# Hedgehog attention and channel mix: the first batch in halves, with four two-bank PSUM tiles and reuse of tiles ahead of the first mix

## The chip, the cores and the metric

The kernel runs on one core of a Trainium2 chip. The metric is the device time in microseconds (us). A kernel is executed several times, in rounds with the kernel before on the same chip. A run more than 1.5% above the fastest of its kernel counts as slow, and slow runs are left out of the comparisons. A difference of 2% or more counts as faster or slower.

Engine names are those of the profile: PE is TensorE's matmuls, PEld its weight loads, DVE is VectorE, ACT ScalarE, POOL GpSimd, SP SyncE (it issues DMAs). "Half clock" is a stretch in which the profile shows a granted TensorE clock of 0.50. In the kernel before, such a stretch lasts 3.41 us, and in it a product of 512 columns starts every 0.427 us, at full clock every 0.216 us (medians, from start to start).

## The reference, cut to what matters

```python
def phi(x):                                   # q, k: (8, 8, 576, 64), w_phi: (64, 128)
    proj = einsum('bhsd,df->bhsf', x, w_phi)
    proj = proj - max(abs(proj), axis=-1)
    return concatenate([exp(proj), exp(-proj)], axis=-1)
kv  = einsum('bhsf,bhsd->bhfd', phi(k), v);   z = sum(phi(k), axis=2)
x   = (phi(q) @ kv) / (phi(q) . z + 1e-6)     # heads side by side: (8, 576, 512)
xk  = mu_k * x + (1 - mu_k) * x_prev          # x_prev: x moved down by one row, zeros first
xr  = mu_r * x + (1 - mu_r) * x_prev
out = sigmoid(xr @ w_r) * (relu(xk @ w_k) ** 2 @ w_v)     # w_k: (512, 1024)
```

There are 8 batches of 4 head pairs, so 32 pairs, numbered 0 to 31. The channel mix of a batch needs x of all its pairs.

## The kernel before: the parts that matter here

The program defines small groups of instructions, each with a name, and one long list, ORDER, gives the sequence in which they are emitted. Each engine's queue has that sequence, and what stands behind a waiting instruction waits too: GpSimd stood idle 2.80 us until a copy could run at 131.54 us, and a cast behind it, whose input VectorE had written by 130.35 us, ran at 133.10 us. `qp4` is the q product of pair 4, `h0.3` the fourth slice of batch 0's first channel-mix product. `:1` gives the PSUM tile, `/DVE` the engine where there is a choice, and `+3@0` puts three dummy matmuls ("fills") in front. These compute nothing and keep PE busy.

The program held eight PSUM banks, as three two-bank tiles ("P") and two single banks ("M"). A sequence has 576 = 9 x 64 rows; the ninth slot of each q and k, the "tail", is worked on its own:

```python
def tp():   s["ps"] = ps = ptile(A, "ps_e")         # a two-bank tile: k tail in bank 0, q tail in bank 1
def rt_():  ...                                     # DVE: maxima of both banks
def mhe():  ...                                     # POOL: maxima as two bf16 parts
def mte():                                          # PE: their transpose, into a single bank M
    s["pm"] = pm = motile(("mo", "m" + tag), "ps_me")
    nc.tensor.transpose(pm[:, 0:64].bitcast(BF), mh, ident)
def mce(eng): copy(eng, s["mT"], s["pm"][:, 0:64].bitcast(BF))
def kae():  nc.tensor.matmul(s["ps"][:, 0, 0:n*128], ...)                # PE: k tail less its maximum
def ekt():  ... nc.scalar.activation(t, s["ps"][:, 0, 0:n*128], Exp)     # ACT: two exponentials, tk
def qte():                                          # PE: the q tail anew, into a single bank M
    s["pq"] = ps = motile(("mo", "q" + tag), "ps_qe")
    nc.tensor.matmul(ps[:, 0:n*128], lhsT=wph[64:128, :], ...)
def eqe():  ... nc.scalar.activation(t, s["pq"], Exp)                    # ACT: two exponentials, tq
# ... cut ...
def eq(pn):                                         # ACT: exponentials of q, two of 512 for each sign
    for h in range(2):
        nc.scalar.activation(t[:, h, :], s["qT"][:, h], AF.Exp, scale=(1.0 if pn == 0 else -1.0))
```

From pair 8 on, x is transposed by a DMA (`xz`, tile `xs<-x_sc`). A small copy (`xu`), a difference (`df`) and two mixes (`xa`, `xb`) follow, on POOL and DVE.

Of the kernel before, what the change touches and what calls it, by code (L numbers as in the profile page):

```python
# [8 lines left out]
FP = mybir.dt.float32  # L9
BF = mybir.dt.bfloat16  # L10
AF = mybir.ActivationFunctionType
ALU = mybir.AluOpType
# [7 lines left out]
ones ident lv0.0 lv0.0.d:0 lk0.1 lq0.1 lv0.1 dve2 hk hq hk.d:0 lk0.1.d:0 dve3 hq.d:0 lk0.0.d/ACT  # L20
lq0.0.d/DVE lk0.2 lq0.2 pt0:2+9@0 wphi wphi.d:0 mus dve1 lv0.2 lk1.0 pb0/DVE pa0/ACT tr0 tp0.0:2+1@0
rt0.0 mhe0.0 lk0.2.d:0 qp0:1 rq0 lq0.2.d:0 kp0:0 rk0 mte0.0:1+3@0 lq1.0 lq1.0.d:0 lv1.0 mh0
lq0.1.d:0 pt1:1 pa1/DVE mce0.0/ACT kae0.0 lk1.2 lq1.2 lv1.2 pb1/ACT tr1 lq1.2.d:0 qp1:1+2@0 mt0:1
rq1 ekt0.0 mc0/ACT wk.0 pt2:2 ka0 pb2/DVE pa2/ACT kp1:1 rk1 mh1 ea0 pt3:2 pb3/ACT lk1.0.d:0 eb0
pa3/DVE tr3 mt1:1+4@0 mc1/DVE tr2 vc0/POOL wk.1 qp2:2 ka1 ea1 mus.d:0 eb1 rq2 kv0:0 kc0/DVE wr.0
wk.1.d:0 wr.1 lv1.2.d:0 kp2:2+1@0 rk2 wv.0 qt0:0 pt4:1+1@0 lv1.0.d:0 mh2 mt2:1+1@0 qa0 qb0 lk1.2.d:0
pa4/DVE pb4/DVE qte0.0:0 eqe0.0 tp0.1:1 mc2/DVE ka2 tr4 lv0.2.d:0 pt5:0 ea2 rt0.1 mhe0.1
mte0.1:0+1@1 pb5/DVE wv.0.d:0 pa5/DVE eb2 mce0.1/DVE kae0.1+2@1 lv0.1.d:0 ekt0.1 pt6:0 pb6/ACT
pa6/DVE pt7:2 pa7/DVE nd0:1 qt1:0 rd0 pb7/ACT vc1/POOL vc2/POOL vc3/ACT qp3:2 rq3 kp3:1+1@1 wv.1 rk3
mh3 tr6 qa1 qb1 tp0.2:2+3@1 qte0.1:0 tr7 eqe0.1 rt0.2 mhe0.2 kv1:0 kc1/ACT xt0:1 xf0/ACT mt3:0  # L30
mc3/ACT nd1:0 tr5 vc4/POOL xe0/ACT ka3 ea3 eb3 df0/POOL mte0.2:1+1@0 rd1 xt1:0 mce0.2/DVE kae0.2
ekt0.2 tp1.0:0 qte0.2:1 eqe0.2 rt1.0 qp4:1 qt2:2 lk2.0 qa2 qb2 mhe1.0 mte1.0:1 rq4 xa0 kv2:1 kc2/ACT
mce1.0/DVE kae1.0 ekt1.0 vc5/POOL xf1/DVE xb0 qte1.0:1 wr.0.d:0 kp4:2 kv3:1 eqe1.0 kc3/ACT nd2:0 rk4
mh4 mt4:1 rd2 qp5:1 mc4/ACT ka4 rq5 xe1/ACT wk.0.d:0 ea4 eb4 lq2.0 xt2:1 lq2.0.d:0 qp6:0 rq6
df1/POOL xa1 qt3:1+1@0 qa3 kv4:2+1@0 kc4/DVE wk.d xb1 wr.1.d:0 kp5:0 qt4:2+1@0 rk5 qb3 nd3:1 rd3 mh5
xe2/ACT mt5:0+3@0 lk2.0.d:0 tr2.0 xf2/ACT xt3:1 qa4 qb4 mc5/ACT df2/DVE ka5 xe3/ACT xf3/ACT tr2.2
xa2 xb2 wv.1.d:0 ea5 eb5 nd4:2 rd4 df3/POOL xa3 qt5:1 qa5 xb3 kv5:0+3@0 tr2.2.d:0 kp6:2 xt4:1
xf4/ACT xe4/DVE kc5/ACT h0.0:0 h0.1:1 qb5 rl0.0/ACT rl0.1/ACT sq0.0/ACT vc6/POOL vc7/DVE rk6 qp7:1
nd5:0 df4/POOL rq7 mh6 mt6:1 mc6/ACT h0.2:0 rl0.2/ACT qt6:1 qa6 xa4 tr2.0.d:0 wr.d r0.0:1 tr9 xb4
sq0.2/POOL th0.0 tr8 rd5 h0.3:0 qb6 sq0.1/POOL rl0.3/DVE lv2.0 lv2.0.d:0 xt5:1 xf5/DVE xe5/DVE ka6  # L40
kp7:0 h0.4:0 h0.5:1 qp8:1 ea6 df5/POOL eb6 rl0.4/ACT sq0.4/ACT rk7 mh7 sq0.3/ACT kv6:2 rl0.5/DVE
mt7:1 mc7/ACT lk3.0 lq3.0 lv3.0 lk4.0 lq4.0 rq8 lk4.0.d:0 kc6/ACT r0.1:0 th0.1 ka7 ea7 eb7 tr11 tr10
lq3.0.d:0 tp2.0:1 rt2.0 h0.6:1 r0.2:0 rl0.6/DVE sq0.6/ACT th0.2 nd6:2 rd6 h0.7:1 mhe2.0 mte2.0:0
mce2.0/DVE vc8/POOL vc9/POOL kv7:0 kc7/DVE rl0.7/ACT vc10/POOL kae2.0 ekt2.0 qp9:2 rq9 qte2.0:1
xt6:0 sq0.7/POOL qt7:0 lk3.0.d:0 xf6/DVE xe6/DVE eqe2.0 qa7 qb7 kp8:1 rk8 kp9:2 rk9 wv.d sq0.5/POOL
v0.0:0 ob0.0 tr3.0 so0.0 mh8 mt8:1 nd7:0 mc8/ACT ka8 mh9 mt9:0 mc9/ACT xa5 tr3.2 xb5 v0.1:1 rd7
ob0.1 tr3.2.d:0 vc11/ACT ea8 df6/POOL eb8 xa6 xb6 v0.2:0 ob0.2 xt7:1 xe7/ACT xf7/ACT qt8:1 qa8 qb8
df7/DVE xa7 xb7 ka9 lv3.0.d:0 vc12/POOL kv8:0 r0.3:0 tr3.0.d:0 tr13 tr12 lq4.0.d:0 th0.3 v0.3:1
kc8/DVE ob0.3 kp10:0 so0.1 qp10:1 rq10 rk10 ea9 eb9 h1.0:0 h1.1:1 rl1.0/ACT sq1.0/ACT nd8:1 rd8
kv9:2 kc9/ACT h1.2:0 qt9:1 qp11:2 mh10 rq11 rl1.1/ACT xz8 rl1.2/ACT sq1.2/POOL mt10:1 so0.2 mc10/ACT  # L50
sq1.1/POOL h1.3:0 rl1.3/DVE qa9 qb9 r1.0:1 th1.0 sq1.3/POOL kp11:2 rk11 mh11 ka10 ea10 h1.4:0 tr15
eb10 lv4.0 rl1.4/DVE sq1.4/ACT h1.5:1 rl1.5/DVE mt11:0 mc11/DVE so0.3 nd9:1 qp12:0 sq1.5/ACT ka11
xz8.d:0 ea11 eb11 h1.6:0 h1.7:1 vc13/POOL vc14/POOL tr14 vc15/POOL rd9 rq12 xz9 qt10:1 xz9.d:0
rl1.7/DVE rl1.6/DVE lk5.0 kv10:2 kc10/DVE tp3.0:0 sq1.7/POOL rt3.0 qa10 mhe3.0 qb10 r1.1:1 th1.1
he0.0:0 rle0.0/DVE nd10:1 r1.2:1 sq1.6/ACT mte3.0:0 mce3.0/ACT rd10 xz10 xz10.d:0 qt11:2 th1.2
kp12:1 xu8/POOL df8/DVE xa8 so0.0.d:0 kae3.0 xu9/POOL qa11 qb11 rk12 v1.0:1 ob1.0 mh12 ekt3.0
he0.1:0 mt12:1 mc12/ACT xb8 kv11:2 lv4.0.d:0 so0.1.d:0 tr4.0 df9/DVE rle0.1/ACT kc11/ACT qp13:0
qte3.0:1 sqe0.0/DVE eqe3.0 xu10/POOL df10/POOL ka12 kp13:2 so0.2.d:0 so0.3.d:0 so1.0 ea12 so1.0.d:0
r1.3:0 eb12 rq13 rk13 nd11:0 rd11 th1.3 v1.1:1 xz11 xz11.d:0 mh13 sqe0.1/ACT xa9 xb9 ob1.1 xa10 xb10
mt13:0 mc13/ACT kv12:0 kc12/ACT ka13 ea13 eb13 qt12:1 qa12 tr4.0.d:0 tr16 vc16/POOL xu11/POOL  # L60
df11/POOL qp14:0 rq14 v1.2:1 ob1.2 qb12 re0:0 the0 kp14:0 rk14 xa11 kv13:2 kc13/DVE so1.1 qt13:1
mh14 xb11 v1.3:0 tr4.2 tr4.2.d:0 tr19 vc17/POOL ob1.3 so1.3 mt14:1 qa13 nd12:2 qb13 mc14/ACT
vc18/POOL qp15:1 rq15 ka14 so1.1.d:0 ea14 so1.2 eb14 lq5.0 rd12 xz12 xz12.d:0 h2.0:0 rl2.0/DVE ve0:1
qt14:2 lq5.0.d:0 obe0 soe0 soe0.d:0 kp15:0 kv14:1 sq2.0/ACT qa14 qb14 lv5.0 lv5.0.d:0 vc19/DVE
h2.1:1 rk15 kc14/ACT h2.2:0 nd13:2 rd13 xz13 xz13.d:0 lk6.0 rl2.1/ACT sq2.1/POOL mh15 rl2.2/ACT
sq2.2/POOL r2.0:1 th2.0 tr18 h2.3:0 so1.3.d:0 mt15:1 tr17 qp16:2 qp17:1 mc15/DVE rl2.3/ACT lq6.0
lv6.0 ka15 ea15 eb15 h2.4:0 h2.5:1 rq16 rq17 sq2.3/POOL rl2.4/ACT xu12/POOL df12/POOL qt15:2 qa15
tp4.0:0 kv15:1 kc15/ACT h2.6:0 sq2.4/ACT rl2.5/DVE rt4.0 mhe4.0 rl2.6/DVE nd14:1 rd14 h2.7:1 qb15
vc20/POOL xa12 sq2.5/POOL lk5.0.d:0 xu13/POOL mte4.0:0 kp16:2 rk16 mce4.0/ACT kp17:1 rk17 kae4.0
mh16 rl2.7/ACT ekt4.0 r2.1:0 r2.2:1 th2.1 mt16:0 mc16/DVE xb12 xz14 df13/DVE nd15:0 so1.2.d:0 rd15  # L70
sq2.6/ACT xz15 sq2.7/ACT lq6.0.d:0 th2.2 mh17 ka16 ea16 xa13 v2.0:0 ob2.0 xb13 tr5.0 tr5.2 tr5.0.d:0
tr20 v2.1:1 eb16 mt17:0 mc17/ACT xz14.d:0 kv16:2 kc16/ACT ob2.1 vc21/POOL vc22/POOL qp18:0 rq18 ka17
ea17 qte4.0:1 xu14/POOL eb17 kp18:2 rk18 v2.2:0 eqe4.0 tr5.2.d:0 tr23 qp19:1 lk6.0.d:0 xz15.d:0
xu15/POOL df14/POOL xa14 qt16:0 qa16 ob2.2 r2.3:1 th2.3 mh18 v2.3:0 rq19 qb16 df15/POOL mt18:1
mc18/ACT kv17:1 so2.0 kc17/ACT xb14 ka18 ea18 eb18 qt17:0 qa17 qb17 nd16:1 xa15 xb15 h3.0:1 ob2.3
rd16 xz16 h3.1:0 rl3.0/DVE sq3.0/POOL so2.3 qp20:1 kp19:2 h3.2:1 rl3.2/ACT so2.2 rl3.1/DVE rk19
so2.2.d:0 r3.0:0 rq20 h3.3:1 th3.0 mh19 sq3.1/ACT sq3.2/POOL vc23/ACT rl3.3/ACT mt19:0 mc19/DVE
nd17:1 r3.1:0 th3.1 sq3.3/ACT so2.0.d:0 tr22 qt18:0 rd17 xz17 xz17.d:0 xz16.d:0 xu16/POOL qa18 qb18
ka19 ea19 df16/POOL xa16 kv18:1 kc18/DVE h3.4:0 rl3.4/DVE lk7.0 tr21 tp5.0:1 rt5.0 h3.5:1 sq3.4/DVE
rl3.5/ACT h3.6:0 rl3.6/DVE eb19 nd18:0 rd18 h3.7:1 mhe5.0 mte5.0:0 xz18 rl3.7/DVE sq3.5/ACT qt19:2  # L80
qp21:0 xu17/POOL rq21 mce5.0/ACT kae5.0 ekt5.0 sq3.6/POOL df17/POOL r3.2:1 th3.2 qte5.0:0 kv19:1
lv6.0.d:0 eqe5.0 kc19/ACT kp20:0 so2.3.d:0 xb16 he1.0:1 sq3.7/DVE v3.0:0 so2.1 xz18.d:0 so2.1.d:0
tr6.0 rk20 mh20 rle1.0/DVE qa19 qb19 xu18/POOL df18/POOL vc24/POOL mt20:1 mc20/DVE kp21:2 ka20
vc25/POOL ob3.0 so3.0 rk21 mh21 he1.1:1 rle1.1/DVE nd19:1 r3.3:0 rd19 xz19 xz19.d:0 mt21:1 ea20 eb20
xa18 qt20:0 mc21/ACT th3.3 qp22:1 xb18 qa20 lq7.0 rq22 ka21 v3.1:0 v3.2:1 ob3.1 kv20:1 qb20 xa17
xb17 ea21 eb21 so3.0.d:0 kc20/ACT ob3.2 so3.2 qt21:2 kv21:0 kp22:1 tr6.2 so3.1 re1:1 tr6.2.d:0
xu19/POOL df19/DVE xa19 sqe1.0/ACT xb19 tr27 rk22 mh22 v3.3:0 ob3.3 kc21/ACT nd20:0 rd20 sqe1.1/POOL
xz20 qa21 qb21 nd21:2 mt22:0 the1 tr6.0.d:0 h4.0:1 tr24 mc22/ACT ka22 ea22 rd21 qt22:0 so3.2.d:0
qa22 rl4.0/DVE ve1:0 eb22 vc26/POOL sq4.0/DVE lv7.0 r4.0:1 th4.0 tr25 obe1 qb22 so3.3 qp23:2 rq23
vc27/POOL xz21 kp23:1 rk23 h4.1:0 rl4.1/ACT xz20.d:0 h4.2:1 rl4.2/ACT h4.3:0 qp24:0 kv22:2 xz21.d:0  # L90
# [881 lines left out]
```

## Time and profile before

| | before |
|---|---|
| time, median | 307.35 us (305.68 to 308.5, 4 runs) |
| profiled execution, span | 304.2 us |
| first channel-mix product starts at | 51.92 us |
| from there to the end | 252.3 us |
| PE idle in the span | 25.8 us |
| half clock | 6.8 us, at 36 and at 135 us |

The page's busy time of each engine, with its share of the span and its count of instructions:

```profile
PE 278.4 (92%) x3765; PEld 158.4 (52%) x3813; DVE 240.3 (79%) x369; ACT 223.3 (73%) x408; POOL 127.4 (42%) x261
```

PE is close to full, so there are two ways to lose time: make PE idle, or make its clock slower, which shows as more busy time for the same work (0.427 us in place of 0.216 for a product, above). The list of waits says who made PE wait (engine, tile, line, releaser: us in all, times, longest):

```profile
PE ps_me L476 <- POOL mhlt L471: 3.5, 3, 2.4
...
PE ps_qT L606 <- ACT tk L490: 0.2, 1, 0.2
```

The second row is the only wait of PE for a tail's exponentials (tk or tq), 0.2 us in all.

### The profile page before, as it was taken

What the parts mean: (1) busy time and instruction counts of PE and PEld (TensorE: products, weight loads), DVE (VectorE), ACT (ScalarE), POOL (GpSimd) and SP (SyncE); (2) the same over time, 40 slices, a digit from 0 to 9 for tenths busy, and PEclk for the clock granted to TensorE, in tenths of its full rate; (3) what the DMA queues carried; (4) which work ended last, traced back from release to release, by engine and by line L of the source; (5) the groups of instructions that cost most, each with busy time, mean ns of one, the idle gap of its engine ahead of it and who ended that gap; (6) DMA issues with size and microseconds to landing.
All of it is one profiled execution on the core that took longest, in us unless ns stands there. A gap on an engine that the chain in (4) does not pass through costs nothing.

```text
span 304.2 us, 9054 instructions
## 1 busy us (share of the span) xinstructions
PE 278.4 (92%) x3765; PEld 158.4 (52%) x3813; DVE 240.3 (79%) x369; ACT 223.3 (73%) x408; POOL 127.4 (42%) x261
## 2 busy tenths in 40 slices
PE   6688798999899999969999997999999999999993
PEld 2456465565456655534555654454556655554541
DVE  5776789979978999667978988799869888777331
ACT  3397899998689897855888884898797878923410
POOL 7763533696047346653443714353034403400400
PEclk9999989999999999998999999999999999999999
DMA  8999957399989957996957898913924364233125
GB/s 152 204 209 207 169 83 105 59 194 206 194 174 128 148 124 131 197 200 113 177 110 107 145 125 157 162 47 61 187 60 69 11 93 94 58 74 71 39 58 116
DMA packets 66137, 38.18 MB, mean 126 GB/s; under 512 B 47024, under 2 KB 60720, under 8 KB 66096
## 3 DMA queue, kind: packets, MB, share of 16 engines
q1 hardware_dynamic: 51280, 20.82, 39.4%
q0 software_dynamic: 14672, 16.48, 35.1%
q8 instruction: 30, 0.49, 0.7%
q10 hardware_dynamic: 144, 0.29, 0.3%
q14 instruction: 11, 0.09, 0.1%
HBM read 33.62 MB, written 9.44 MB: 142 GB/s over the span
## 4 chain that ended last, share of the span: by engine, by line
PE 61%; DVE 18%; DMA 7%; ACT 6%; issue 3%; POOL 2%; SPq 1%; DVEq 0%; POOLq 0%
PE ps_v L812 14%; PE ps_h L779 13%; PE ps_r L798 7%; PE ps_nd L656 5%; DMA xs<-x_sc 4%; PE ps_kv L635 4%; DVE nm L565 4%; DVE nm L560 3%; DVE xk L706 2%; PE ps_ve L896 2%; ACT q L620 2%; PE ps_he L866 2%; DVE xr L706 2%; PE ps_q L548 2%; PE ps_k L598 2%
## 5 line engine op out<-in xcount | busy, mean ns | idle before, releaser
L620 ACT ACTIVATE q<-ps_qT 128x512 bf16<-128x512 f32 x128 | 67.1, 622 | 3.0 <-PE ps_qT L612 2.8
L575 ACT ACTIVATE k<-ps_k 128x1024 bf16<-128x1024 f32 x64 | 62.9, 1038 | 5.6 <-PE ps_k L598 4.3
L779 PE MATMUL ps_h<-xk,wk_bf 128*128 128x512 bf16 x237 | 60.8, 379 | 1.3 <-issue 0.3
L812 PE MATMUL ps_v<-wv_bf,kk 128*128 128x512 bf16 x243 | 58.2, 379 | 1.0 <-issue 0.3
L565 DVE TENSOR_REDUCE nm<-ps_q 128x8 f32<-128x1024 f32 x32 | 38.7, 1218 | 4.3 <-PE ps_q L548 4.1
L560 DVE TENSOR_REDUCE nm<-ps_k 128x8 f32<-128x1024 f32 x32 | 38.8, 1217 | 3.8 <-PE ps_k L548 3.8
L812 PEld LDWEIGHTS <-kk 128*128 128x128 bf16 x256 | 23.9, 98 | 28.8 <-issue 1.9
L211 POOL TENSOR_TENSOR kk<-krelu 128x512 bf16<-128x512 bf16 x23 | 23.9, 1047 | 35.4 <-DVE krelu L205 21.7
L779 PEld LDWEIGHTS <-wk_bf 128*128 128x128 bf16 x256 | 22.5, 97 | 25.2 <-issue 2.3
L584 POOL CAST mhl<-nm 128x16 bf16<-128x16 f32 x32 | 8.0, 250 | 64.1 <-DVE nm L560 64.0
L798 PE MATMUL ps_r<-wr_bf,xr 128*128 128x512 bf16 x118 | 32.9, 394 | 1.2 <-issue 0.5
L804 ACT ACTIVATE rt<-ps_r 128x512 bf16<-128x512 f32 x32 | 19.5, 609 | 18.0 <-PE ps_r L798 15.7
L700 POOL TENSOR_TENSOR diff<-xs 128x576 bf16<-128x576 bf16 x21 | 28.0, 1336 | 7.6 <-DVE xs L682 2.8
L203 ACT ACTIVATE krelu<-ps_h 128x512 bf16<-128x512 f32 x39 | 23.2, 611 | 10.1 <-PE ps_h L779 8.3
L706 DVE SCALAR_TENSOR_TENSOR xk<-diff,mu_k_t,xs 128x576 bf16<-128x576 bf16 x32 | 28.5, 892 | 1.3 <-POOL diff L700 1.0
L818 DVE SCALAR_TENSOR_TENSOR ob<-rt,ps_v 128x512 f32<-128x512 bf16 x32 | 21.8, 682 | 8.7 <-PE ps_v L812 4.2
L666 DVE TENSOR_TENSOR x_sc<-ps_nd,rden 128x640 bf16<-128x640 f32 x32 | 26.4, 825 | 1.1
L706 DVE SCALAR_TENSOR_TENSOR xr<-diff,mu_r_t,xs 128x576 bf16<-128x576 bf16 x32 | 26.9, 840 | 0.0
L548 PEld LDWEIGHTS <-qkT 64*128 64x128 bf16 x512 | 17.6, 94 | 12.0 <-issue 9.7
L635 PE MATMUL ps_kv<-v,k 64*128 64x65 bf16 x1024 | 22.8, 192 | 0.6 <-ACT q L620 0.4
L635 PEld LDWEIGHTS <-k 64*128 64x128 bf16 x1024 | 19.9, 95 | 5.1 <-issue 3.8
L205 DVE TENSOR_SCALAR krelu<-ps_h 128x512 bf16<-128x512 f32 x25 | 17.1, 688 | 6.6 <-PE ps_h L779 6.0
(99 smaller groups left out, 467.5 us busy)
## 6 DMA issues: line engine op xcount, KB each, us to landing
out_dram<-ob SPq DMA_DIRECT2D x72, 128.0 KB, 2.4
nat<-in_k_dram POOLq DMA_DIRECT2D x6, 576.0 KB, 8.6
nat<-in_q_dram POOLq DMA_DIRECT2D x6, 576.0 KB, 8.9
vt<-in_v_dram POOLq DMA_DIRECT2D x6, 576.0 KB, 9.6
wk_bf<-in_moe_w_k_dram POOLq DMA_DIRECT2D x2, 512.0 KB, 10.8
wv_bf<-in_moe_w_v_dram POOLq DMA_DIRECT2D x2, 512.0 KB, 12.3
nat<-in_k_dram POOLq DMA_DIRECT2D x3, 288.0 KB, 7.4
nat<-in_q_dram POOLq DMA_DIRECT2D x3, 288.0 KB, 7.3
```

What stands on the lines that cost most here:

```text
L211: (nc.vector if eng == "DVE" else nc.gpsimd).tensor_tensor(out_, in_, in_, op=ALU.mult)
L560: nc.vector.tensor_reduce(s["nm"][:, 0, :], s["k"].rearrange("p a (g f) -> p (a g) f", f=128), axis=AX.X, op=ALU.max, apply_absolute_value ...
L565: nc.vector.tensor_reduce(s["nm"][:, 1, :], s["q"].rearrange("p a (g f) -> p (a g) f", f=128), axis=AX.X, op=ALU.max, apply_absolute_value ...
L575: nc.scalar.activation(s[f"k{pn}"], s["k"].rearrange("p a (g f) -> p (a g) f", f=128), AF.Exp, scale=(1.0 if pn == 0 else -1.0))
L620: nc.scalar.activation(t[:, h, :].rearrange("f (g a p) -> f g a p", g=4, a=2), s["qT"].rearrange("f a (g h p) -> f h g a p", g=4, h=2)[:, ...
L635: nc.tensor.matmul(ps[:, hh, pn * 65:(pn + 1) * 65], lhsT=s[f"k{pn}"][r, c, :], rhs=vb[r, a, 2 * g + par, :], start=(pn == 0 and c == 0), ...
L666: nc.vector.tensor_tensor(s["x"].rearrange("p (b s) d -> p b s d", b=2), ndv[:, :, :, 0:64], s["rd"].to_broadcast([128, 2, 5, 64]), op=ALU ...
L700: (nc.vector if eng == "DVE" else nc.gpsimd).tensor_tensor(s["d"], xs[:, a, 64:64 + S], xs[:, a, 0:S], op=ALU.subtract)
L706: nc.vector.scalar_tensor_tensor(out=t[:, a, (b % 2) * S:(b % 2 + 1) * S], in0=s["d"], scalar=mu[:, a:a + 1], in1=xs[:, a, 0:S], op0=ALU.m ...
L779: nc.tensor.matmul(ps, lhsT=wk_bf[:, c, fc * 128:(fc + 1) * 128], rhs=xkt[bp][:, c, m0:m0 + 512], start=(c == 0), stop=(c == NDC - 1))
L798: nc.tensor.matmul(ps, lhsT=xrt[bp][:, c, m0 + ci * 128:m0 + (ci + 1) * 128], rhs=wr_bf[:, c, :], start=(c == 0), stop=(c == NDC - 1))
L812: nc.tensor.matmul(ps, lhsT=s["kk"][:, fc, ci * 128:(ci + 1) * 128], rhs=wv_bf[:, fc, :], start=(fc == 0), stop=(fc == NFC - 1))
```

## The change

The intent is to start the channel mix earlier, by working the first batch in two halves of its q slots from the exponentials to the mix, and by giving the attention of the first 50 us a fourth two-bank tile. For that tile the two single banks are given up until the channel mix begins, so what lay in them goes into tiles that are held anyway.

```diff
+    early = ExitStack()                                   # a fourth two-bank tile until the first single bank is asked for
+    def ptile(i, name):
+        return (pools["P"] if i == 3 else psum).tile([128, 2, 512], FP, name=name, tag=f"P{i}")
     def fill(n, i):
-        t = psum.tile([128, 512], FP, name="ps_f", tag=f"M{i}")
+        t = ptile(i, "ps_f")                              # fills need a two-bank tile as well
 ... tails ...
-            s["pm"] = pm = motile(("mo", "m" + tag), "ps_me")
-            nc.tensor.transpose(pm[:, 0:64].bitcast(BF), mh, ident)
+            nc.tensor.transpose(s["ps"][:, 1, 0:64].bitcast(BF), mh, ident)
-            s["pq"] = ps = motile(("mo", "q" + tag), "ps_qe")
+            s["pq"] = ps = s["ps"][:, 1, :]               # bank 1 of the tail's own tile
 ... pairs ...
-            s["pm"] = motile(("mo", "m" + N), "ps_m")
+            s["pm"] = s["q"][:, 0, :] if n < NMQ else motile(("mo", "m" + N), "ps_m")     # NMQ = 6
-                for h in range(2):                        # two exponentials of 512
-                    nc.scalar.activation(t[:, h, :]..., s["qT"]...[:, h], AF.Exp, ...)
+                nc.scalar.activation(t..., s["qT"]..., AF.Exp, ...)     # one of 1024
-            ps = motile(("mo", "x" + N), "ps_x")
+            s["px"] = px = s["nd"][:, 0, :].bitcast(BF)
+        if n < NHALF:                                     # pairs 0 to 3: qt, qa, qb, nd, rd, xt, xe, df, xa, xb twice
+            for i, h in enumerate("yz"): ...
 ... casts of the maxima may go to DVE; more buffers for exponentials, kv, x, relu ...
 ORDER: all words arranged anew; fills 39 -> 15; casts of 20 of 32 pairs and of 3 of 10 tails on DVE
```

## The prediction

> **What bounds the kernel now.** I read the map of the span in 40 slices first, then the busy time by stretch, then the order of instructions around the first channel mix, then the chain that ended last. From the map, the TensorE row and its clock:
>
> ```profile
> PE   6688798999899999969999997999999999999993
> PEclk9999989999999999998999999999999999999999
> ```
>
> A slice is 7.6 us. PE is not full in the first seven slices, and after that only in slice 18 (about 130 to 138 us), in slice 25 and in the last one. The table by stretch puts numbers to it (columns: stretch, length, busy us of PE, weight loads, DVE, ACT, POOL with their counts, clock, DMA share, GB/s):
>
> ```profile
> 10.00:40.00 30.00, 23.24 (x426) 16.34 (x429) 21.46 (x34) 24.23 (x50) 16.80 (x40) 0.94 1.09 185
> 40.00:52.60 12.60, 11.16 (x214) 6.96 (x214) 11.98 (x18) 11.59 (x24) 4.80 (x7) 1.00 0.79 108
> 60.00:300.00 240.00, 229.97 (x3018) 128.55 (x3057) 193.97 (x283) 178.10 (x320) 94.16 (x191) 0.99 0.73 120
> ```
>
> From 60 to 300 us PE is busy 96%: that part is PE-bound. From 10 to 40 us no engine is full (PE 77%, DVE 72%, ACT 81%), so waits between engines bound it; from 40 to 52.6 DVE (95%) and ACT (92%) do. And the head's PE share is flattered by dummy matmuls on `ones`[...] (second row below; 39 in the order, 34 of them recorded): 39 x 0.216 us = 8.4 us, all before 52 us. The head ends where the channel mix can first feed PE (order of time; start, length, then what):
>
> ```profile
> 50.67 1.19 DVE L706 SCALAR_TENSOR_TENSOR xk<-diff,mu_k_t,xs 128x576 bf16<-128x576 bf16 x1 [0.18 <-POOL diff L700]
> 51.92 2.10 PE L779 MATMUL ps_h<-xk,wk_bf 128*128 128x512 bf16 x7
> L287 PE MATMUL ps_f<-ones 128*128 128x512 bf16 x34 | 12.0, 449 | 1.5 <-DVE ones L251 1.5
> ```
>
> The first `ps_h` starts 0.06 us after the mix of the fourth head pair ends (50.67 + 1.19 = 51.86). From there to the end 304.2 - 51.9 = 252.3 us pass, almost all PE-bound. So a microsecond saved before 51.9 comes out at the end, if PE still has the same work left. The one large hole later is this, from the chain and from PE's list:
>
> ```profile
> 125.10 13.39 DMA xs<-x_sc
> ...
> 134.53 0.23 PE L476 MATMUL ps_me<-ident,mhlt 128*128 128x128 bf16 x1 [2.44 <-POOL mhlt L471]
> ```
>
> A transpose by DMA, whose median landing is 3.5 us, took 13.39 us; POOL stood in front of a copy that waits for it, the small casts for the tails stood behind that copy, and PE stood idle for 2.44 us.
>
> [...]granted clock 0.63 and 0.52 from 36 to 40 us, and 0.50 for some 3.3 us from 135.6, right after the 2.44 us hole. [...]Before: three two-bank tiles and two single ones[...]; after, until the channel mix, four two-bank tiles. [...]The 13.39 us transpose falls in a stretch (121 to 140 us) of DMA share 1.1 to 1.3 with five loads of 576 KB issued from 117.5 to 127 us[...].
>
> **The change part by part.**
>
> *q exponentials of pairs 4 to 31:* two of 512 become one of 1024. In the trace four of 512 in a row take 2.06 us, two of 1024 take 1.94: 0.12 us a pair, 28 x 0.12 = 3.4 us of ACT. ACT is 74% busy after 60 us, so nearly all of that lies beside PE work.
>
> *Pairs 0 to 3 in halves.* PE gets the same columns in more instructions, hidden. ACT gets 16 exponentials of 512, as before. DVE gets 6- and 4-slot normalisations, copies and mixes of 256 and 64 columns. A mix of 576 takes 0.81 us, 0.73 of it to the next start; [...]0.40 for 256 columns, 0.20 for 64 (estimates from this trace). Split mixes cost 0.27 us more a pair each, about 2 us over eight, normalisations about 0.4 us a pair more. So DVE gets more work in the batch, but the first channel-mix product needs only the first halves.
>
> *DVE up to the first possible product.* The changed program's DVE list from the first transpose copy to the last first-half mix, priced by start-to-start times of the trace: 13 wide reductions x 1.13 = 14.7; 3 small ones 1.3; 11 transpose copies x 0.40 = 4.4; 5 pairs of casts now on DVE x 0.25 (a guess; they are POOL's before) = 1.25; 5 small copies x 0.17 = 0.85; normalisations 4 x 0.70 + 4 x 0.58 = 5.1; 7 copies to `xs` x 0.24 = 1.7; one `kv` and one difference 0.6; 11 mixes of 256 = 4.4; 3 of 64 = 0.6. Sum 34.9 us. The kernel before had DVE busy 35.69 of the 45.9 us from 6.7 to 52.6 us, 78%. So the work ahead of the first product is no smaller; all depends on the waits. What cuts them: a fourth two-bank tile; the q tile of a pair takes the transposed maxima, and the tails use their own tile (no single bank to wait for); the casts of the maxima go from POOL to DVE behind the reduction that makes them (POOL's reaction and 0.5 us go from the chain of pairs 0 to 3 and 5); shorter links in halves; more buffers for exponentials, x, kv. The fill matmuls fall from 39 to 15, so the schedule expects fewer holes. I take 85% for DVE: 6.7 + 34.9 / 0.85 = 47.8 us for the first product, which is 4.1 us earlier. ACT by the same count has 33.4 us from 4.8 on: at 85% 44.1 us, not the last.
>
> *What PE has left then.* In the changed order the first product (`ps_r`, then `ps_h`) comes before the k projection of pair 6, `kv` of pair 5 and the transposes of pair 4; before they came ahead of it and took 50.75 to 51.92 = 1.2 us. Gain of the head: 4.1 - 1.2 = 2.9 us.
>
> *The hole at 132 us.* It costs 2.44 us and half of 3.3 us of slow clock: 4.1 us. The new order spreads these five loads more (over 239 words of the order, from q of batch 5 to v of batch 6, where it was 47), and 20 of 32 casts leave POOL. But other transposes meet loads elsewhere, so I count half: 2.0 us.
>
> *The rest* of the order is new throughout, with the same instructions; I count 0. Sum: 2.9 + 2.0 = 4.9 us. From the mean of the three runs before, 307.4, that is 302.5; from the profiled run, 306.0, it is 301.1. I take 302.0.
>
> **The rivals.**
> - *DVE stays the bound of the head.* For it: 95% from 40 to 52.6, and the sum is not smaller. If the share of busy time stays 78%, the first product is at 6.7 + 44.7 = 51.4 us, the 1.2 us eat the gain: about 306.
> - *A new stall in the middle.* For it: a fixed order cannot know when a DMA lands, and all engines take their lists in order, so one late transpose stops POOL and then PE. One such hole with its clock dip is 4 us: 305 to 307, slower if there are two. Against it: more buffers (exponentials 3, relu 4, x 4, kv 3), so more slack.
> - *The head fills almost fully.* With DVE at 95% the first product is at 43.4 us, 4.4 earlier than I take it; with the clock dip at 36 to 40 us gone as well: about 297.
> - *ACT becomes the bound.* With the q exponentials of batch 0 unmerged its sum is 33.4 us, below DVE's: against.
>
> **Range and chances.** The head can give between 0 and 7 us, the middle between -2 and +4. Low 297.0, high 306.5. Two per cent of 307.4 is 301.3; my number lies just above it, so faster by over 2% 0.42, within 2% 0.53, slower 0.05.
>
> **What would show it.** First channel-mix product between 46 and 50 us, and DVE busy over 24 of the 30 us from 10 to 40 (was 21.46): the head as I see it. No clock below 0.9 from 30 to 45 us. Exponentials `q` of 1024 columns at about 1038 ns. No idle of PE over 2 us between 60 and 290 us, and no `xs<-x_sc` over 8 us on the chain. PE busy about 24 x 0.216 = 5 us less, being fills. Wrong if the first product comes after 51 us, or if it comes early and PE's idle time after 60 us (10 us before) grows by as much.

2.9 us for the head and 2.0 us for the hole at 132 us are 4.9 us, 302.5 us from the mean of the rounds and 301.1 us from the profiled run, taken as 302.0. Half the length of a slow stretch as its price is an estimate, from the 0.427 and 0.216 us above; the 1038 ns for 1024 columns is the mean of the k exponentials in the trace of before (622 ns for q's of 512). The prices of 0.40 us for a mix of 256 columns and 0.20 us for one of 64 were worked out with a rate that is cut, but the trace of before gives about the same. There a maximum over 1024 columns takes 1.22 us and one over 256 takes 0.43 us, 768 columns in 0.79 us. By this rate 576 columns are 0.59 us of the 0.73; with the rest held fixed, that gives 0.40 and 0.20 us (an estimate). The split normalisations (0.70 and 0.58 us) were estimates too; in the kernel after they take 0.70 and 0.55 us.

## The result, and the profile after

| | before | after |
|---|---|---|
| time, median | 307.35 us | 327.78 us (325.12 to 329.23, 4 runs) |
| ratio | | 1.066, 95% interval 1.0570 to 1.0749: slower |
| span of the profiled execution | 304.2 us | 326.5 us |
| first channel-mix product | 51.92 us | 53.41 us |
| from there to the end | 252.3 us | 273.1 us |
| PE busy / idle | 278.4 / 25.8 us | 288.1 / 38.4 us |
| half clock | 6.8 us | 44.4 us |

A ratio here and below is the mean time of one kernel's fast runs over that of the other's of the same rounds, so it is not quite the ratio of the medians that I quote.

The page after, its busy times and its map of PE and PE's clock in 40 slices (8.2 us each here):

```profile
PE 288.1 (88%) x3784; PEld 164.9 (51%) x3829; DVE 250.4 (77%) x431; ACT 230.7 (71%) x373; POOL 121.8 (37%) x214
...
PE   6766869996989849998999989899999989999993
...
PEclk9996767997899958999999979999999979999999
```

Two readings follow. PE's idle time grew by 12.6 us. PE's busy time grew by 9.7 us although 24 fills of 0.216 us are gone (5.2 us), and the clock row tells why: six dips where before there were two. PE was busy for 36.3 us within the six dips, before for 6.4 us within the two. If all work takes twice as long at half clock, as nearly the products of 512 columns do (0.427 against 0.216 us from start to start in this trace too), half of the difference, 15.0 us, is the price (an estimate). That makes up the 9.7 + 5.2.

Where the time came in is shown by the table by stretch (length, then busy us of PE, PEld, DVE, ACT, POOL, clock, DMA share, GB/s), before and after:

```profile
60.00:120.00 60.00, 58.19 (x858) 34.12 (x866) 53.91 (x75) 50.16 (x91) 32.29 (x62) 1.00 1.03 160
```

```profile
60.00:120.00 60.00, 49.41 (x704) 30.16 (x710) 47.24 (x68) 40.71 (x65) 28.11 (x43) 0.90 0.79 127
```

PE was busy in 97% of the stretch from 60 to 120 us before; after, it stands idle in it for 10.6 us instead of 1.8, at a lower clock. The first product, for which all was done, is 1.5 us later, not 4.1 earlier:

```profile
53.41 2.08 PE L957 MATMUL ps_r<-wr_bf,xr 128*128 128x512 bf16 x7
```

The list of PE's waits after has a new first row, and the second is the largest single hole:

```profile
PE ps_e L508 <- ACT tk L503: 6.7, 6, 1.2
PE ps_e L496 <- DVE mTe L206: 5.0, 2, 4.7
```

The first is the tail's q product waiting for the tail's **k** exponentials, which it does not use. In PE's and ACT's order of time at one of the six places:

```profile
187.31 0.39 PE L496 MATMUL ps_e<-sel,mTe 64*128 64x512 bf16 x1
188.87 0.37 PE L508 MATMUL ps_e<-qkT,wph 64*128 64x512 bf16 x1 [1.17 <-ACT tk L503]
```

```profile
187.74 1.08 ACT L503 ACTIVATE tk<-ps_e 128x512 bf16<-128x512 f32 x2 [0.32 <-PE ps_e L496]
189.50 1.09 ACT L518 ACTIVATE tq<-ps_e 128x512 bf16<-128x512 f32 x2 [0.68 <-PE ps_e L512]
```

PE writes bank 0 (L496), ACT reads bank 0 twice (two exponentials, 1.08 us), and only then does PE write bank 1 of the same tile (L508). The second row of the waits is this piece of the chain that ended last (start, length, what):

```profile
106.77 9.79 DMA xs<-x_sc
...
116.61 0.24 POOL xs L206
...
116.92 0.04 DVE diff L712
116.96 0.34 issue
117.30 0.23 DVE mTe L206
...
117.57 0.62 PE ps_e L496
```

DVE stood in front of pair 9's difference, which waits for a transposing DMA of 9.79 us. The copy of a tail's maxima (`mTe`), whose input PE had written by 112.26 us, stood behind it in DVE's queue, and PE needed that copy.

### The profile page after: what moved, and what is told of

Read it like the earlier page. It is cut to its first block, busy times and chain, and to the rows that moved or that the text cites. A ratio compares the mean times of both kernels' runs of the same rounds, so it can differ in the third digit from the quotient of the medians.

```text
span 326.5 us, 9047 instructions
## 1 busy us (share of the span) xinstructions
PE 288.1 (88%) x3784; PEld 164.9 (51%) x3829; DVE 250.4 (77%) x431; ACT 230.7 (71%) x373; POOL 121.8 (37%) x214
## 4 chain that ended last, share of the span: by engine, by line
PE 59%; DVE 25%; ACT 6%; DMA 5%; issue 3%; POOL 0%; SPq 0%; DVEq 0%
PE ps_v L971 14%; PE ps_h L938 12%; PE ps_r L957 6%; DVE nm L576 5%; PE ps_nd L669 4%; DMA xs<-x_sc 4%; PE ps_kv L649 4%; DVE nm L581 3%; PE ps_k L614 2%; PE ps_q L564 2%; DVE x_sc L679 2%; PE ps_ve L1058 2%; PE ps_qT L622 2%; PE ps_k L564 2%; ACT tk L503 2%
## 5 line engine op out<-in xcount | busy, mean ns | idle before, releaser
L971 PE MATMUL ps_v<-wv_bf,kk 128*128 128x512 bf16 x244 | 62.5, 400 | 1.0 <-issue 0.4
L635 ACT ACTIVATE q<-ps_qT 128x1024 bf16<-128x1024 f32 x56 | 54.6, 1028 | 6.2 <-PE ps_qT L628 6.0
L938 PE MATMUL ps_h<-xk,wk_bf 128*128 128x512 bf16 x204 | 52.1, 380 | 1.6 <-issue 0.6
L712 POOL TENSOR_TENSOR diff<-xs 128x576 bf16<-128x576 bf16 x22 | 30.3, 1376 | 19.7 <-DVE xs L695 9.3
L210 ACT ACTIVATE krelu<-ps_h 128x512 bf16<-128x512 f32 x44 | 26.0, 601 | 11.3 <-PE ps_h L938 9.5
L938 PEld LDWEIGHTS <-wk_bf 128*128 128x128 bf16 x224 | 19.6, 97 | 22.7 <-issue 2.1
L206 POOL COPY xs<-xs 128x63 bf16<-128x63 bf16 x20 | 5.9, 295 | 54.0 <-DMA xs<-x_sc 54.0
L718 DVE SCALAR_TENSOR_TENSOR xk<-diff,mu_k_t,xs 128x576 bf16<-128x576 bf16 x28 | 24.4, 872 | 0.3 <-POOL diff L712 0.2
L679 DVE TENSOR_TENSOR x_sc<-ps_nd,rden 128x640 bf16<-128x640 f32 x28 | 23.1, 824 | 1.0
L564 PEld LDWEIGHTS <-qkT 64*128 64x128 bf16 x512 | 17.6, 98 | 10.2 <-issue 7.0
L669 PE MATMUL ps_nd<-kv,q 128*128 128x65 bf16 x448 | 19.8, 199 | 0.0
```

What stands on the lines that cost most here:

```text
L564: nc.tensor.matmul(ps[:, par, g * 128:(g + 1) * 128], lhsT=qkT[b][r, g0 + gg + g, :], rhs=wph[r, :], start=(g == 0), stop=(g == 3))
L635: nc.scalar.activation(t.rearrange("f j (a p) -> f j a p", a=2), s["qT"].rearrange("f a (j p) -> f j a p", p=64), AF.Exp, scale=(1.0 if pn ...
L669: nc.tensor.matmul(ps[:, bk, o * 65:(o + 1) * 65], lhsT=tail if sl < 2 else s[f"q{pn}"][:, sl - 2, :], rhs=s["kv"][:, sl % 2, pn, :], star ...
L712: pick(eng).tensor_tensor(s["d"], xs[:, a, 64:64 + S], xs[:, a, 0:S], op=ALU.subtract)
L718: nc.vector.scalar_tensor_tensor(out=t[:, a, (b % 2) * S:(b % 2 + 1) * S], in0=s["d"], scalar=mu[:, a:a + 1], in1=xs[:, a, 0:S], op0=ALU.m ...
L938: nc.tensor.matmul(ps, lhsT=wk_bf[:, c, fc * 128:(fc + 1) * 128], rhs=xkt[bp][:, c, m0:m0 + 512], start=(c == 0), stop=(c == NDC - 1))
```

## The experiments

Seventeen kernels ran, all correct. I quote the medians, with the ratio to the kernel before of the same rounds.

### First: three parts mended in the kernel after

My readings were the tails' waits, the missing fills (clock), and the casts that had gone to DVE, where some took long:

```profile
95.73 1.80 DVE L601 TENSOR_TENSOR mhl<-nm,mhl 128x16 bf16<-128x16 f32 x1
```

**a_tails**: the tail's q product is put directly beside its k product, ahead of the k exponentials. Nothing else moves. (In tails 0.0, 0.1, 1.0 and 6.0 the q product already stood ahead of the k exponentials; in the first three of them the k product moves up to it. The other six are the six waits.)

```diff
- ... kae0.2 ekt0.2 ... qte0.2 ...        (bank 0 written, bank 0 read, bank 1 written)
+ ... kae0.2 qte0.2 ekt0.2 ...            (both written, then read); side by side in all ten tails
```

> Changed kernel (327.8 us), only the order of words edited: for every tail the q product (ps_e, second bank) stands directly beside the k product, so that PE no longer waits for the exponentials of the k tail, which read the first bank of the same tile. Theory 'tails': the six waits of PE on those exponentials (6.7 us in all) go, and with them at least the two short slow-clock stretches at 190 and 265 us (3.4 us each at half clock, so 1.7 us each): 317 to 321 us. Rival 'PE only waits elsewhere' (the exponentials still have to run before kv): 325 to 328 us.

**a_fills**: 30 fills added in the head where a tile is dead (45 in all).

```diff
- kv1:2  mt2  qty1:1  qte0.2  ...  kae1.0  ...
+ kv1:2+2@1  mt2+2@1  qty1:1+2@3  qte0.2+3@0  ...  kae1.0+4@2  ...      (13 places)
```

> Changed kernel with 45 dummy matmuls in the head in place of 15 (the kernel before has 39), each before a product that waited and on a tile that is free there; nothing else. Theory 'clock': the two stretches of 10.2 us at half clock (26.5 to 36.7 and 43.4 to 53.6) shrink to at most one of 3.4 us, the first channel-mix product comes 3 to 6 us earlier than 53.4 us, and the time is 319 to 324 us. Rival 'the head is bound by DVE and ACT, so that its clock does not matter': first product at 53 us or later, time 326 to 330 us.

**a_pool**: all 23 casts on DVE back to POOL.

```diff
- mh0/DVE  mh1/DVE ... mhe2.0/DVE ...
+ mh0/POOL mh1/POOL ... mhe2.0/POOL ...
```

> Changed kernel with all casts of the maxima on POOL again (23 words changed from DVE to POOL), order of words kept. Theory 'casts': the small casts on DVE, up to 1.8 us each beside POOL's work, stood between the maxima and PE; without them 321 to 325 us. Rival 'POOL waits for transposes by DMA with the casts behind them': no gain or a loss, 327 to 332 us, with PE idle released by POOL casts.

**a_three**: all three.

> All three edits at once. If tails, clock and casts are the causes and roughly add: 305 to 313 us. If what is left is the new order itself (a transpose of 9.8 us at 107 us with 4.7 us of idle PE), it stays at 315 us or more.

| kernel | median us | ratio | first product |
|---|---|---|---|
| after | 327.78 | 1.0660 | 53.41 |
| a_tails | 316.71 | 1.0371 | 51.94 |
| a_fills | 334.65 (two of four runs slow, the profiled one too; the fast two 329.11 and 333.07) | 1.0845 | 57.83 |
| a_pool | 327.32 | 1.0733 | 56.46 |
| a_three | 328.89 | 1.0769 | 63.39 |

The tails are 9 to 11 us of the loss: 11.1 us by the medians, which come from different rounds, and 8.8 us by the ratios (1.0660 less 1.0371, of 306 us). The row of tail waits is no longer in PE's list, and half clock falls from 44.4 to 27.3 us. The casts are not the cause, and moving them brings nothing: PE then waits for POOL instead, up to 2.62 us at 21.89 us. The fills make it worse. A fill needs a two-bank tile of its own here, and stood waiting for one (this trace is of a slow run, but the fast runs are slower than the kernel after as well):

```profile
40.27 0.38 PE L297 MATMUL ps_f<-ones 128*128 128x512 bf16 x1 [1.43 <-ACT k L587]
```

Two of my three theories fell.

### Second: single parts put into the kernel before

**b_tails**: the tails' maxima and q product in bank 1 of their own tile, q product behind the k exponentials.

```diff
-            s["pq"] = ps = motile(("mo", "q" + tag), "ps_qe")
+            s["pq"] = ps = s["ps"][:, 1, :]          (and mte, mce likewise)
- ... kae0.0 ... ekt0.0 ... qte0.0:0 eqe0.0
+ ... kae0.0 ... ekt0.0 qte0.0 eqe0.0
```

The edit moves words too: in the kernel before, the q product and its exponentials stood some words after the k exponentials; here they follow directly, and the tile of tail 1.0 is asked for a little later.

> Kernel before, with this one part of the change: the tails keep their maxima and their q product in the second bank of their own tile, with the q product after the exponentials of the k tail, as the changed order has it for tails of batches 2 to 7. Theory 'tails': PE waits 1.1 to 1.2 us for those exponentials at each tail of a whole batch and 0.4 to 0.8 us at the small ones, 8 to 10 us of waits with one or two more stretches of slow clock: 312 to 318 us. Rival 'other work of PE fills the wait': 305 to 308 us.

**b_tails_q**: the same, with two words exchanged, `kae qte ... ekt eqe`.

> As b_tails, but with the q product before the exponentials of the k tail (the same tiles, only the two words swapped). Theory 'it is the order of the two within one tile, not the tile': 303 to 309 us, within 1% of the kernel before. Rival 'keeping one two-bank tile for the whole tail costs': 309 us or more.

**b_fills15**: 15 of the 39 fills, as many as the kernel after has.

> Kernel before with 15 of its 39 dummy matmuls, the number of the changed kernel, all of them before 11 us; nothing else. Theory 'clock': stretches at half clock in the head grow from 3.4 us to 7 us or more, the first channel-mix product comes 1 to 4 us later than 51.9 us, time 307 to 311 us. Rival 'the dummies do not matter': one stretch of 3.4 us or none, 303 to 306.5 us.

**b_exps**: the merged q exponentials alone.

```diff
-                for h in range(2):
-                    nc.scalar.activation(t[:, h, :]..., s["qT"]...[:, h], AF.Exp, ...)
+                nc.scalar.activation(t..., s["qT"]..., AF.Exp, ...)
```

> Kernel before with its q exponentials merged, 64 of 1024 columns in place of 128 of 512; nothing else. By the prediction's sum ACT gets 64 x 0.065 = 4.2 us less work, nearly all beside PE work: 303 to 306 us, a gain of up to 2 us. Rival: the order, tuned for the two halves, stumbles over it: slower by up to 1%.

| kernel | median us | ratio (95%) | first product | from there on |
|---|---|---|---|---|
| before, same rounds | 305.97 | 1 | 51.92 | 252.3 |
| b_tails | 320.01 | 1.0470 (1.0421 to 1.0519) | 57.63 | 258.9 |
| b_tails_q | 309.19 | 1.0104 (1.0066 to 1.0141) | 52.64 | 255.4 |
| b_fills15 | 307.87 | 1.0064 (1.0000 to 1.0128) | 55.01 | 253.1 |
| b_exps | 305.13 | 0.9965 (0.9914 to 1.0016) | 50.53 | 251.1 |

(The last two columns are of each kernel's profiled execution.) The tails' wait is now shown in both directions: taking it out of after gave 9 to 11 us; with it the kernel before took 14.0 us longer, and exchanging the two words, which is all that b_tails_q changes in b_tails, gave back 10.8 of these. The waits list of b_tails has the row of the kernel after:

```profile
PE ps_e L490 <- ACT tk L485: 9.9, 9, 1.3
```

The 10.8 us are a little more than the sum of the nine waits (9.9 us). A dip of the clock went with them: half clock is 13.7 us in b_tails, and 6.8 in b_tails_q as in before. The runs show that the wait is there when the two banks are one tile of the program, and what it costs. None ran without the guard, so whether the chip needs this wait is not shown; in b_tails_q the order of words removes it lawfully. What b_tails_q still loses (3.2 us) goes with the tile that is held longer: PE now waits for the q tail's exponentials to free it, for instance 1.29 us at 39.46 us. How much of it the moved words cost, no run separates.

### Third: what the other 11 us are

**a_tails_whole**: a_tails with the first batch whole again, at the place of the later half.

```diff
-    NHALF = NP
+    NHALF = 0                                  (and the row offsets that go with it)
- qtz0:3 ... qty0:0 ... ndy0:2 rdy0 ... ndz0:1 rdz0 ...
+            ... qt0:0  ...             ... nd0:1 rd0 ...      (so for pairs 0 to 3; r0.0, th0.0, r0.1, h0.0, th0.1 behind xb3; sq0.6 ahead of v0.0)
```

> The kernel after with its tails mended (316.7 us, 1.037 of before), and in it the first batch whole again: one q product, one pair of exponentials, one numerator, one transpose and one mix of 576 columns for each head pair, where the two halves were, at the place of the later half. The r and h products of the first two column blocks stand behind the last mix; all else is as it was. Theory 1, the halves are worth what I predicted of them (their products start some 4 us earlier, at the price of about 1 us more work): the first channel-mix product comes at 54 to 56 us where it was 51.94, and the time is 319 to 321. Theory 2, in this order the halves bring nothing, because the first product waits for the last half mix of the last pair, which is as late as the whole one: 315 to 318, first product within 1 us. Theory 3, they cost more than they bring (DVE was busy for 36.0 of the 42 us from 10 to 52): 312 to 315, and DVE is busy less in this stretch.

It took 327.26 us, ratio 1.0702 (1.0637 to 1.0768), where a_tails had 316.71 and 1.0371: without the halves 10.1 us more by the ratios, 10.6 by the medians. PE's first `ps_r` starts at 62.99 instead of 51.94 us, and then waits within it for the last pair's mix:

```profile
66.95 2.31 PE L949 MATMUL ps_r<-wr_bf,xr 128*128 128x512 bf16 x5 [2.41 <-DVE xr L710]
```

Theory 1 holds in kind: in this order the first product starts 11 us earlier with the halves, not 4. Not all of that is shorter links. Ahead of its first product a_tails_whole ran 31.1 us at half clock, a_tails 17.1, so up to half of the 14.0 us between them may be the clock; and the order was made for halves. Yet a_tails is no earlier than before. So something in the head takes as much as the halves give.

**hyb_whole** looks for it: the parts of the change but the halves and the casts on DVE, in the order of the kernel *before*.

```diff
 the program of after, with NHALF = 0
 ORDER of before; qte directly behind kae, eqe behind ekt; tiles 0 to 3 given out anew
- ... kv1 ... qp5 ... qt4 ... nd3 ... kp6 ...
+ each some words later, where one of the four tiles is free; 26 of 39 fills
```

> The program of the kernel after with the first batch whole (no halves), in the order of the kernel before: four two-bank tiles until the first channel-mix product, tails and transposed means and transposed x in their own tiles, merged exponentials, GpSimd casts as before; each tail's q product directly behind its k product; tiles given out anew, five groups of words (kv1, qp5, qt4, nd3, kp6) moved a few words back to where a tile comes free; 26 of the 39 fills, where a tile is dead. Theory 1, the order of the kernel after costs the rest: the parts cost here what they cost alone in before (own tiles +3.2, merged exponentials -1.1, 13 fills fewer some +1): 308 to 311 (1.006 to 1.017), and the first channel-mix product comes within 2 us of before's 51.92. Theory 2, the parts cost it, since tiles are held longer and four two-bank tiles are fewer places than three and two single banks: 314 to 318 (1.025 to 1.04), with waits of PE for ScalarE or VectorE to free tiles in the first 60 us.

It took 331.51 us (one of six runs slow), ratio 1.0832 (1.0779 to 1.0885), worse than either theory. Its first product:

```profile
69.33 1.04 PE L931 MATMUL ps_h<-xk,wk_bf 128*128 128x512 bf16 x4
```

That is 17.4 us later than before; from there to the end it needs 257.1 us, 4.8 more than before. In the head PE waits again and again for ACT to free a tile, and the clock goes with it (from 40 to 69 us it is 0.59 in the mean):

```profile
33.07 0.29 PE L462 MATMUL ps_e<-wph,qkT 64*128 64x128 bf16 x4 [2.01 <-ACT q L628]
...
47.45 0.62 PE L642 MATMUL ps_kv<-v,k 64*128 64x65 bf16 x16 [1.73 <-ACT tq L511]
```

So in both orders that were tried, four two-bank tiles, held longer for the tails, maxima and transposes, went with a later first product than three with two single banks, as long as the batch is whole. That the tiles are the cause is not shown alone: I moved the words by hand, 13 fills are gone as well, and some of those left wait for tiles too. But a_tails_whole, in the order of after, is nearly as late (62.99 us, and stopped until 66.95).

**What is left after the first product.** a_tails needs 264.5 us from there on (316.4 - 51.9), before 252.3, hyb_whole 257.1. The windows from the first product to the end, before and in a_tails, divide the 12.2 us:

```profile
51.92:304.20 252.28, 237.86 (x3095) 132.60 (x3135) 201.46 (x295) 185.23 (x334) 98.84 (x197) 0.99 0.71 118
```

```profile
51.94:316.40 264.46, 242.11 (x3177) 137.17 (x3218) 207.46 (x327) 194.55 (x306) 94.87 (x151) 0.98 0.64 110
```

PE is idle for 22.35 us instead of 14.42, so 7.9 us are waits. It is busy for 4.2 us more. Of these about 3.0 are the clock (PE busy 9.3 us in dips, before 3.2; half of the difference, an estimate), and the 1.2 us left fit the work that before had done ahead of its first product. The two largest holes of PE in a_tails are at 113 us (4.54, as the chain above) and at 206 us (2.89). Five runs went after them. Each takes waiting instructions out of the way of others:

```diff
 a_tails_mend   - df9/DVE  mce3.0/DVE          + df9/POOL mce3.0/ACT;  xa20 xb20 behind rd22
 a_tails_mend2  a_tails_mend, and              + xu9 df9 behind mh12;  xa9 xb9 behind rd11
 a_tails_loads  a_tails, and                   + loads lv4.0 lk5.0 behind mh12
 a_mend_loads   a_tails_mend, and              + loads lv4.0 lk5.0 behind mh12
```

> The kernel after with its tails mended, and two engine queues mended as well: the difference of pair 9 is on GpSimd and the copy of the fourth tail's mT on ScalarE, so that VectorE doesn't stand behind the transposing transfer before PE's 4.54 us hole at 113 us; and the two mixes of pair 20 stand behind the next two numerators' divisions, so that VectorE frees their tiles first (PE's 2.89 us hole at 206 us). Theory 1, these two holes are time that nothing gives back: 4.5 + 2.9 us less, and up to 3.4 us of half clock at 113 and at 205 us gone as well (half of that is lost time: 1.7 each): 306 to 310. Theory 2, holes only move: some wait in the same place ends 1 to 2 us earlier and the time is 313 to 316. In either case the holes at 113 and 206 are below 1.5 us in the trace if the edits do what they should.

> a_tails_mend (315.56 us, 1.0334), and now pair 9's copy and difference stand behind the casts of pair 12 on GpSimd, its two mixes behind the numerator's division of pair 11 on VectorE. Theory 1, the copies that wait for transposing transfers are what is left of the loss: the hole of 5.95 us before 113.27 us falls below 2 us, and 4 to 6 us go with it: 309 to 312 (1.012 to 1.022). Theory 2, the wait moves on once more, or its time was slack: 314 to 316.

> The kernel after with its tails mended (316.7 us), and the loads of v and k of the fifth batch, which GpSimd issued at about 99.7 and 100.5 us, just in front of pair 9's transposing transfer, issued behind GpSimd's work of pair 12 instead (their data are wanted only some 30 us later). Theory 1, the loads are what made that transfer 9.8 us long: it falls below 6 us, PE's hole of 4.54 us at 113 us below 2 us, and 3 to 5 us go: 312 to 314 (1.020 to 1.028). Theory 2, the transfer is short but another wait takes its place: 315 to 317. Theory 3, the transfer stays as long without the loads, since it waits in the queue for the two transposes in front of it: 316 to 317, hole unchanged.

> The same on a_tails_mend (315.56 us, hole of 5.95 us at 113.27 us). Theory 1: the hole below 2 us and 310 to 312 (1.013 to 1.020), the best of the kernels made from the one after, and still slower than before by the half clock of the head and its later start. Theory 2 and 3: 314.5 to 316.

| kernel | median us | ratio (95%) | PE's longest holes after 60 us |
|---|---|---|---|
| a_tails | 316.71 | 1.0371 (1.0317 to 1.0425) | 4.54 at 113, 2.89 at 206 |
| a_tails_mend | 315.56 (one of four runs slow) | 1.0334 (1.0266 to 1.0402) | 5.95 at 113 |
| a_tails_mend2 | 317.27 | 1.0371 (1.0329 to 1.0412) | 3.46 at 117, 2.07 at 207 |
| a_tails_loads | 316.46 | 1.0377 (1.0313 to 1.0441) | 3.11 at 122, 3.68 at 202 |
| a_mend_loads | 315.10 | 1.0306 (1.0231 to 1.0382) | 3.11 at 123, 1.60 at 73 |

The intervals overlap: no clear gain. The traces say where the hole went, one line from each of a_tails_mend, a_tails_mend2 and a_tails_loads:

```profile
113.27 0.29 PE L600 MATMUL ps_m<-ident,mhl 128*128 128x128 bf16 x1 [5.95 <-POOL mhl L596]
```

```profile
117.23 0.39 PE L617 MATMUL ps_qT<-qkT,wph 64*128 64x512 bf16 x2 [3.46 <-DVE nm L576]
```

```profile
122.49 0.29 PE L600 MATMUL ps_m<-ident,mhl 128*128 128x128 bf16 x1 [3.11 <-POOL mhl L596]
```

First it was behind DVE's copy; then, with the difference on POOL, behind POOL's casts; with both moved, behind DVE's mixes. Two loads of 576 KB, issued at about 99.7 and 100.5 us, had made these transfers long. From issue to landing, those of pairs 9 and 10 took, in a_tails and then, with the two loads moved, in a_tails_loads:

```profile
DMA to landing us min/median/max: 8.8/9.2/9.7
```

```profile
DMA to landing us min/median/max: 2.6/2.6/2.7
```

But the next transfer, of pair 11, meets the loads instead: 9.90 us from 109.92, on the chain of a_tails_loads, where it took 2.6 in a_tails. Theory 2 (another wait takes the place) holds in kind in all four.

### Fourth: the same in the kernel before, and a version that beats both

```diff
 b_moves     + xu12 df12 behind mhe4.0;  df19 xa19 xb19 behind ob3.3
 b_both      b_moves and the merged exponentials
 b_exps_xu   merged exponentials;  xu12 df12 behind mhe4.0;  xu13 behind mh17, df13 ahead of xa13
```

> The kernel before, with two groups of instructions moved in the same manner: GpSimd's copy and difference of pair 12 behind the fifth tail's casts (GpSimd stood idle 2.80 us at 131.5 for their transfer and the casts waited behind them), and VectorE's difference and mixes of pair 19 behind the next two outputs (VectorE idle 2.51 us at 183.9 for the same reason). PE's holes near 133 to 138 and at 187.8 should shrink. Theory 1, they are time on the path: 1 to 3 us less, and the half clock at 135 us gone: 302 to 305 (0.988 to 0.997). Theory 2, a later wait takes their place: within 0.5 us of before.

> The kernel before with the two moves and with the change's merged q exponentials (0.9965 alone). If the two gains lie in different places they add: 301 to 304 (0.983 to 0.994), better than both kernels. If the moves bring nothing: 0.996, as with the exponentials alone.

> The kernel before with merged q exponentials (0.9965), GpSimd's copy and difference of pair 12 behind the fifth tail's casts, and now the copy of pair 13 behind the casts of pairs 16 and 17 and its difference in front of its mixes. Theory 1, b_moves failed only because the copy of pair 13 stood in the way of the casts: PE's 2.44 us hole at 134 us goes and the 5.25 us of b_moves doesn't come: 301 to 304 (0.984 to 0.993). Theory 2, the stretch from 125 to 140 us is bounded by the transposing transfers themselves (13 to 14 us each), so the wait comes back elsewhere: 305 to 308.

b_moves took 309.36 us (1.0087, interval 1.0045 to 1.0129) and b_both 310.35 (1.0116, 1.0067 to 1.0164): both a little slower, against both theories. The reason is again the next instruction in the queue. POOL's copy for pair 13 now stood in front of the casts, and its transfer took 14.21 us:

```profile
125.78 14.21 DMA xs<-x_sc
...
140.05 0.23 POOL xs L195
```

```profile
140.81 0.28 PE L585 MATMUL ps_m<-ident,mhl 128*128 128x128 bf16 x1 [5.25 <-POOL mhl L581]
```

b_exps_xu moves that copy too, and leaves pair 19 alone. It took **302.83 us, ratio 0.9920 (0.9888 to 0.9953)**: faster than both kernels, if by less than 2%. The transfers of pairs 12 and 13 are as long as ever in it (10.3 and 13.1 us), but fewer instructions stand behind them: PE's longest hole from 120 to 180 us is 0.94 us, and no slice has a low clock. How much the moves add to the merged exponentials isn't settled: the intervals of b_exps and b_exps_xu overlap, and the profiled execution of b_exps has no half clock either. The map of b_exps_xu:

```profile
PE   6789798999899999998999998999999999999993
...
PEclk9999999999999999999999999999999999999999
```

## Why the prediction was wrong

The prediction was 302.0 us, range 297 to 306.5, with 0.05 for slower. It was slower by 6.6%. Its steps, one by one:

- **"the tails use their own tile (no single bank to wait for)": the step that failed worst.** I booked it as a wait removed. It was a wait added: in this program the writer of a tile's second bank waits for the readers of the first (6.7 us in six waits in after, 9.9 us in nine in b_tails). 9 to 11 of the 20 us are this (a_tails), and even in the good order the kernel with the shared tile is 3.2 us slower (b_tails_q). The order of words was open to me, and the tail's `ekt` ahead of `qte` could be read there.
- **"a fourth two-bank tile" as a cut of waits: not borne out.** I counted the tile that came and not the two single banks that went. With all such parts but no halves the first product came at 69.33 us (hyb_whole) against 51.92, though that kernel has a hand-made order and fewer fills too.
- **"shorter links in halves": right, and undersized.** I predicted 4.1 us for the head as a whole. Within the order of after, the first product is 11.1 us earlier with the halves (62.99 to 51.94), a part of it through the clock. The net gain of the head is zero in a_tails, since they only pay back what else in the head got slower, and -1.5 us in after.
- **"I take 85% for DVE: 6.7 + 34.9 / 0.85 = 47.8 us": nearly right for DVE, wrong for the first product.** DVE was busy for 24.7 of the 30 us from 10 to 40 (I said over 24). The last two first-half mixes of the kernel after:

```profile
49.88 0.47 DVE L808 SCALAR_TENSOR_TENSOR xk<-diff,mu_k_t,xs 128x256 bf16<-128x256 bf16 x1
50.27 0.47 DVE L808 SCALAR_TENSOR_TENSOR xr<-diff,mu_r_t,xs 128x256 bf16<-128x256 bf16 x1
```

From start to start, as I had priced it, a mix of 256 columns takes 0.39 us (predicted 0.40), and one of 64 takes 0.20 (0.20); a pair of casts on DVE takes 0.30 in the head (0.25). The last mix ends at 50.74 us. Up to there DVE was busy for 36.4 us (34.9), which is 83% (85): 3.0 us late. The other 2.7 us of the miss (50.74 to 53.41) are a step that I left out. Four groups of products (`qp6`, `ka5`, `qt5`, `nd4`) stood ahead of `r0.0` in PE's queue and ran first, from 50.49 us on, at a granted clock of 0.50.
- **"The fill matmuls fall from 39 to 15, so the schedule expects fewer holes": wrong.** A fill now needs one of the two-bank tiles, which is likely why they fell (not tested). Half clock in the head was 10.2 us from 26.5 and 10.2 from 43.6 us. In before, 24 fills fewer cost about 2 us (b_fills15, whose interval just touches 1; half clock in the head is 17.1 us in its profile, 3.4 in that of before), and putting fills into after made it worse, since they wait for tiles.
- **The hole at 132 us, "I count half: 2.0 us": wrong.** It went, and a hole of 4.65 us at 117.57 us came. My rival "a new stall in the middle" had the mechanism to the letter, and a price of 4 us each. It happened, beside a loss that I had not listed. I had also named the wrong transfer for the old hole. The one of 13.39 us landed at 138.49 us, after PE's hole had ended (134.53). POOL's copy was held up by the transfer of the pair before, 11.0 us from 120.48, and ran at last here:

```profile
131.54 0.23 POOL L199 COPY xs<-xs 128x63 bf16<-128x63 bf16 x1 [2.80 <-DMA xs<-x_sc]
```

- **"The rest of the order is new throughout ... I count 0": wrong.** After the first product a_tails needs 12.2 us more than before: 7.9 of waits, about 3.0 of clock, 1.2 of work done later (I had estimated 1.2). The parts in before's order need 4.8 more there (hyb_whole). The other 7.4 us go with the new order, as far as two kernels with so different a head can be compared. Its two largest holes are tied to transposing transfers; that loads lengthened them is shown for the first. This is shown as far as each edit moved a hole; no edit won the time back. Whether another order with the same parts would, stays open.
- **The q exponentials: right.** 1028 ns in the mean for 1024 columns (predicted 1038). Alone they are worth 0.9965, with an interval that includes 1: they lie beside PE's work, as said.

Of what should have shown it, "PE busy about 5 us less" failed by 15 us through the clock alone. Both signs of being wrong came: the first product after 51 us (53.41), and more idle time of PE after 60 us, 24.9 us to the end of the span (326.5 - 60 - 241.64 busy) against 14.2 before (304.2 - 60 - 229.97; the prediction's 10 us stop at 300).

On the clock: no long gap of PE stood ahead of the first dip. From 26.5 to 36.7 us the kernel after ran at half clock, and between 14 and 43 us no idle of PE was over 0.82 us. Four us before the dip PE was busy 2.69 of 4.00 us:

```profile
22.00:26.00 4.00, 2.69 (x72) 2.01 (x69) 3.71 (x7) 3.25 (x7) 3.56 (x6) 1.00 1.13 214
26.00:30.00 4.00, 2.84 (x27) 1.46 (x28) 2.88 (x5) 3.60 (x8) 2.21 (x7) 0.56 1.22 202
```

But a low busy share alone doesn't foretell a dip here. The kernel before was busy 2.66 of 4.00 us from 10 to 14 us, and the kernel after 2.53 of 4.00 from 16 to 20, both with the clock at 1.00 for more than 6 us after. So the runs give no measure of how much idling is too much. I had looked only for long holes.

## What to carry to other kernels

When two results are moved into one buffer to save a place, ask who reads the first part at the moment the second is written: a place saved can be a wait made, and putting both writes ahead of both reads may take most of it away (10.8 of 14.0 us in b_tails). Count the buffers given up along with those won, and don't book an order that is new throughout at zero: in a fixed order one late transfer stops whichever queue its consumer stands in (GpSimd for 5.82 us until 116.61 us in the kernel after), and moving that consumer pays only if the next one in the queue isn't waiting for the next transfer (b_both against b_exps_xu, which differ in pairs 13 and 19).
